# Decode attention and feed-forward on one core: V of a row's last layer-0 pair used as the matmul's weight, and small PSUM results moved to the score and output banks around each turn

## The chip, the cores and the metric

The kernel runs on one core of one Trainium2 chip. The metric is the device time of one execution in microseconds.

The names used below: PE is TensorE, which multiplies; DVE is VectorE and ACT is ScalarE, which turn its results into the next inputs; PSUM is the memory into which PE writes, in banks of 512 columns. In a product one operand is the weight (`lhsT` in the code) and the other moves (`rhs`).

## The reference, cut to what matters

```python
# B = 8 rows, one query each, D = 640; 32 heads, 4096 cached keys, Dh = 128; Dff = 1728; bf16
x = x + A(layernorm(x))     # "layer 0": attention over the cache, then wo
x = x + F(layernorm(x))     #            feed-forward, relu
x = x + A(layernorm(x))     # "layer 1": the same weights and the same cache again
x = x + F(layernorm(x))
# A: q = x @ wq; p = softmax(q k^T * Dh**-0.5); (p v) @ wo
```

The cache of one row is read twice, and layer 1 of a row can start only when its layer-0 feed-forward is done. 1 GB of K and V has to pass through the core's SBUF.

## The kernel before: the parts that matter

Heads are taken in pairs, 16 pairs per row and layer; one visit is one pair. A pair's K and V are four 512 KB units each. A planner in Python lays down one order of all instructions. An arena of 26 units holds what is loaded. At the end of a row's layer 0, 21 units are kept for layer 1 and three more are stashed, so that they are not read twice; loads near a turn therefore come as single units, issued as units come free. Two pairs of the next row are put between a row's last layer-0 pair and its first layer-1 pair, to give the feed-forward chain time (for the last row, two layer-1 pairs of the row before). I call that stretch the turn. There are eight.

```python
visits += nxt[:AHEAD] + cur + nxt[AHEAD:]         # AHEAD = 2: two pairs of the next row, then layer 1 of this one
...
# after the V products of visit i
ops.append(("OC", i))                             # ACT copies the output bank
step()                                            # at most 20 chain products between two units
chains.append([(6, ("OG", i)), (0, ("O", i))])    # gather; scale by 1/sum
if last_of[layer, b] == i and (layer == 0 or b == B - 1):
    chains[-1] += [(14, ("W", i)), (0, ("YC", i))] + finish(layer, b)
...
def finish(layer, b):     # layer 0: up x5, var, relu, down x5, add, mean, center, query, var2, query
```

Three PSUM banks do all the work; the other five hold the stash.

```python
o_ps = ps.tile([P, CJ * Dh], FP32, name="o_ps")       # output bank
s_ps = ps.tile([P, BANK], FP32, name="s_ps")          # score bank
small_ps = ps.tile([P, BANK], FP32, name="small_ps")  # everything else, by columns:
# oy_ps, sum_ps, mean_ps, var_ps, turn_ps, max_ps, q1_ps, lsum_ps, ffn_ps, P_ps

# do_mm, V: P is the weight, V moves (4 products of 512 columns per unit); only the very last visit has V as weight
nc.tensor.matmul(o_ps[32 * c : 32 * c + CJ, :], lhsT=P_tiles[i][:, h, j : j + CJ],
                 rhs=arena[:, at + c * CJ * Dh : at + (c + 1) * CJ * Dh], ...)
# do_mm, K around a turn: K is the weight, 16 products of one column per unit
s_tiles[i] = s_ps[:, i % 2 * 2 * NJ : (i % 2 + 1) * 2 * NJ]
```

## Time and profile before

| | before |
|---|---|
| median of the first three runs | 2345.71 us (2343.61 to 2347.46) |
| profiled span | 2343.2 us |
| bytes, mean rate | 988 MB, 423 GB/s |
| PE / DVE / ACT busy | 60% / 21% / 18% |

From the page of before: the span, the busy times, the rate in 40 equal slices, the chain that ended last by engine, and the group of ACT's output copies (count, busy us, mean ns, idle before).

```profile
span 2343.2 us, 42314 instructions
PE 1401.7 (60%) x18396; PEld 583.6 (25%) x18396; DVE 495.1 (21%) x2014; ACT 430.1 (18%) x994; POOL 59.6 (3%) x296
...
GB/s 411 430 432 402 431 431 432 431 407 435 430 431 428 412 434 433 432 426 409 431 435 430 423 409 436 429 432 415 416 434 431 432 410 424 431 431 431 393 433 330
...
DMA 70%; PE 18%; ACT 6%; DVE 4%; issue 2%; SPq 0%; DVEq 0%; ACTq 0%; POOL 0%; POOLq 0%
...
L787 ACT CAST o_sb<-o_ps 100x512 bf16<-100x512 f32 x255 | 149.4, 586 | 266.3 <-PE o_ps L679 265.5
```

The rate line is the one to look at. It is flat near 432 GB/s except for eight dips and the first and last slices: the loads bound the kernel, and the dips are the turns. Stretches of 20 us around the fourth turn (columns: busy us and count of PE, PEld, DVE, ACT, POOL; clock; DMA share; GB/s):

```profile
1020.00:1040.00 20.00, 13.46 (x142) 4.28 (x138) 4.43 (x17) 2.89 (x6) 0.00 (x0) 0.50 1.00 427
1040.00:1060.00 20.00, 14.10 (x263) 8.35 (x263) 8.38 (x35) 3.26 (x8) 0.00 (x0) 0.50 1.00 412
1060.00:1080.00 20.00, 16.08 (x342) 11.65 (x343) 4.74 (x28) 2.83 (x11) 4.88 (x23) 0.50 0.99 385
1080.00:1100.00 20.00, 15.47 (x310) 9.42 (x310) 5.86 (x25) 8.72 (x21) 0.00 (x0) 0.50 1.02 425
```

The DMA share stays near 1.00 while the rate falls to 385, so the share is no measure of loss here; the rate is. Summing (1 - rate/432) over the turns gives some 32 us in all.

What PE waits for in a turn, from the view of waits (who, line and tile it writes <- whom: us in total, times, longest us):

```profile
PE s_ps L697 <- ACT P_sb L753: 13.2, 14, 1.1
PE small_ps L572 <- DVE lsum L779: 2.5, 8, 0.3
PE small_ps L792 <- DVE xc L594: 1.8, 7, 0.3
PE small_ps L816 <- ACT qo L655: 1.7, 7, 0.2
PE small_ps L487 <- DVE s1h L481: 2.3, 7, 0.8
```

The last one is the mean's wait for its own input. Counts of 7 and 8 (and 14, twice per turn: 0.76 us in most turns and 1.09 us at the scores of a layer-1 pair just after) say that these come once per turn. The same waits in place, in the timeline of PE in the fourth turn (start us, us, what, and in brackets the idle before it and its releaser):

```profile
1063.86 0.57 PE L697 MATMUL s_ps<-qo,arena 128*128 128x1 bf16 x16 [0.76 <-ACT P_sb L753]
...
1069.51 0.60 PE L679 MATMUL o_ps<-arena,P_sb 128*4 128x512 bf16 x4
1070.04 0.23 PE L773 MATMUL small_ps<-P_sb,few 128*128 128x64 bf16 x1
1070.59 0.60 PE L572 MATMUL small_ps<-hT,w_sb 128*128 128x1 bf16 x14 [0.32 <-DVE lsum L779]
1071.12 0.60 PE L679 MATMUL o_ps<-arena,P_sb 128*4 128x512 bf16 x4
1071.97 0.36 PE L487 MATMUL small_ps<-s1h,few 128*128 128x1 bf16 x2 [0.25 <-DVE s1h L481]
1072.59 0.24 PE L792 MATMUL small_ps<-few,o_sb 100*128 100x2 bf16 x4 [0.26 <-DVE xc L594]
1072.76 0.60 PE L679 MATMUL o_ps<-arena,P_sb 128*4 128x512 bf16 x4
...
1074.16 0.41 PE L816 MATMUL small_ps<-oT,wo_sb 128*128 128x1 bf16 x10 [0.25 <-ACT qo L655]
1074.49 0.60 PE L679 MATMUL o_ps<-arena,P_sb 128*4 128x512 bf16 x4
1075.68 0.60 PE L679 MATMUL o_ps<-arena,P_sb 128*4 128x512 bf16 x4 [0.44 <-DMA arena<-in_A_kv_dram]
```

Each L679 line is one unit of V used, and so one unit of the arena given back to the loads. Units leave here every 1.2 to 1.7 us; at 432 GB/s a 512 KB unit takes 1.21 us. Look at the line at 1070.59: a down product of the feed-forward writes columns 392 to 396 of the small bank (the end of ffn_ps, behind the up products) and waits until DVE has read the softmax sums in columns 216 to 279 of the same bank. No value passes between them. That is the kind of wait the change is after.

### The profile page before, as it was taken

Reading aid. Unit: us, or ns where it says so; the run is one execution under the profiler, and the core shown is the slowest. Engines: PE = TensorE matmul, PEld = TensorE weight load, DVE = VectorE, ACT = ScalarE, POOL = GpSimd, SP = SyncE. Lnnn points to the kernel's source line nnn. Section 1 sums busy time; section 2 is a strip of 40 time slices with the busy share of each in tenths; the row PEclk is TensorE's granted clock in tenths of the full one; section 3 lists DMA queues with packets and bytes.
Section 4 is the critical chain, followed back from the end, with each engine's and each line's share of the span. In section 5 each row is a group of like instructions: output and inputs, shape, how many; then the busy total and the mean of one; then the engine's idle time right before and its main releaser. Section 6 shows DMA issues by size and latency. Waiting matters only on the chain.

```text
span 2343.2 us, 42314 instructions
## 1 busy us (share of the span) xinstructions
PE 1401.7 (60%) x18396; PEld 583.6 (25%) x18396; DVE 495.1 (21%) x2014; ACT 430.1 (18%) x994; POOL 59.6 (3%) x296
## 2 busy tenths in 40 slices
PE   3547655576555855557545685556755577555766
PEld 1214211142112511124111241113311133111523
DVE  1113211131112211122111221112211122111312
ACT  1111211122111221112111121111311112111211
POOL 0000000000000000000000000000000000000000
PEclk9999999999955555555555555555555555555555
DMA  9999999999999999999999999999999999999997
GB/s 411 430 432 402 431 431 432 431 407 435 430 431 428 412 434 433 432 426 409 431 435 430 423 409 436 429 432 415 416 434 431 432 410 424 431 431 431 393 433 330
DMA packets 75598, 990.82 MB, mean 423 GB/s; under 512 B 8468, under 2 KB 8468, under 8 KB 36372
## 3 DMA queue, kind: packets, MB, share of 16 engines
q1 hardware_dynamic: 75412, 988.12, 99.4%
q8 instruction: 143, 2.34, 0.4%
q14 instruction: 43, 0.35, 0.0%
HBM read 988.08 MB, written 0.01 MB: 422 GB/s over the span
## 4 chain that ended last, share of the span: by engine, by line
DMA 70%; PE 18%; ACT 6%; DVE 4%; issue 2%; SPq 0%; DVEq 0%; ACTq 0%; POOL 0%; POOLq 0%
DMA arena<-in_A_kv_dram 70%; PE o_ps L679 5%; PE s_ps L687 4%; PE s_ps L697 3%; ACT P_row L747 2%; PE small_ps L647 1%; ACT o_sb L787 1%; DVE mrow L705 1%; ACT P_sb L753 1%; PE small_ps L792 1%; ACT arena L626 1%; PE small_ps L760 1%; PE small_ps L816 1%; ACT nmax L745 1%; DVE hmx L724 0%
## 5 line engine op out<-in xcount | busy, mean ns | idle before, releaser
L679 PE MATMUL o_ps<-arena,P_sb 128*4 128x512 bf16 x4080 | 598.6, 596 | 407.2 <-DMA arena<-in_A_kv_dram 405.5
L687 PE MATMUL s_ps<-arena,qz 128*4 128x512 bf16 x3040 | 409.7, 601 | 255.9 <-DMA arena<-in_A_kv_dram 245.0
L679 PEld LDWEIGHTS <-P_sb 128*4 128x4 bf16 x4080 | 111.1, 88 | 533.1 <-issue 517.4
L705 DVE TENSOR_REDUCE mrow<-s_ps 100x1 bf16<-100x512 f32 x190 | 131.9, 694 | 354.7 <-PE s_ps L687 354.7
L787 ACT CAST o_sb<-o_ps 100x512 bf16<-100x512 f32 x255 | 149.4, 586 | 266.3 <-PE o_ps L679 265.5
L745 ACT ACTIVATE nmax<-small_ps 100x1 f32<-100x1 f32 x106 | 18.2, 171 | 798.6 <-PE small_ps L734 798.6
L697 PE MATMUL s_ps<-qo,arena 128*128 128x1 bf16 x4224 | 141.3, 165 | 33.9 <-DMA arena<-in_A_kv_dram 17.8
L697 PEld LDWEIGHTS <-arena 128*128 128x128 bf16 x4224 | 129.7, 104 | 50.6 <-DMA arena<-in_A_kv_dram 33.7
L767 DVE CAST P_sb<-small_ps 128x64 bf16<-128x64 f32 x190 | 42.6, 224 | 466.1 <-PE small_ps L760 466.1
L687 PEld LDWEIGHTS <-qz 128*4 128x4 bf16 x3040 | 62.1, 84 | 305.0 <-issue 286.1
L760 PE MATMUL small_ps<-few,P_row 100*128 100x16 bf16 x760 | 52.4, 180 | 96.7 <-ACT P_row L747 96.7
L745 ACT ACTIVATE nmax<-small_ps,q_scale 100x1 f32<-100x1 f32 x84 | 21.9, 261 | 410.8 <-PE small_ps L734 410.8
L779 DVE TENSOR_REDUCE lsum<-small_ps 128x2 f32<-128x64 f32 x256 | 57.5, 225 | 167.8 <-PE small_ps L773 167.8
L719 DVE TENSOR_REDUCE diag<-small_ps 1x2 bf16<-1x16 f32 x190 | 30.8, 162 | 276.9 <-PE small_ps L712 273.2
L760 PEld LDWEIGHTS <-P_row 100*128 100x128 bf16 x760 | 35.2, 108 | 191.9 <-ACT P_row L747 187.1
L647 PE MATMUL small_ps<-xq,wq_sb 128*128 128x1 bf16 x1280 | 51.9, 165 | 40.3 <-DVE qo L807 33.5
L792 PEld LDWEIGHTS <-o_sb 100*128 100x128 bf16 x1020 | 47.9, 107 | 109.0 <-ACT o_sb L787 78.4
L792 PE MATMUL small_ps<-few,o_sb 100*128 100x2 bf16 x1020 | 67.2, 170 | 10.9 <-DVE xc L594 1.8
L747 ACT ACTIVATE P_row<-s_ps,nmax 100x512 bf16<-100x512 f32 x106 | 72.9, 687 | 3.4
L712 PE MATMUL small_ps<-few,mrow 100*1 100x16 bf16 x190 | 35.7, 188 | 55.5 <-DVE mrow L705 55.5
L647 PEld LDWEIGHTS <-wq_sb 128*128 128x128 bf16 x1280 | 53.2, 104 | 53.4 <-issue 51.7
L747 ACT ACTIVATE P_row<-s_ps,nmax,q_scale 100x512 bf16<-100x512 f32 x84 | 65.3, 777 | 2.8
(212 smaller groups left out, 854.6 us busy)
## 6 DMA issues: line engine op xcount, KB each, us to landing
arena<-in_A_kv_dram SPq DMA_DIRECT2D x126, 4096.0 KB, 23.1
arena<-in_A_kv_dram SPq DMA_DIRECT2D x89, 2048.0 KB, 20.4
arena<-in_A_kv_dram SPq DMA_DIRECT2D x218, 512.0 KB, 6.1
arena<-in_A_kv_dram SPq DMA_DIRECT2D x16, 3072.0 KB, 22.0
arena<-in_A_kv_dram SPq DMA_DIRECT2D x38, 1024.0 KB, 10.6
arena<-in_A_kv_dram SPq DMA_DIRECT2D x10, 2560.0 KB, 19.9
arena<-in_A_kv_dram SPq DMA_DIRECT2D x15, 1536.0 KB, 20.5
wq_sb<-in_A_wq_dram SPq DMA_DIRECT2D x4, 1280.0 KB, 17.6
```

The lines of the kernel that those rows point to most:

```text
L647: nc.tensor.matmul(q_ps[:, h : h + 1], lhsT=wq_sb[:, g, c, (2 * n + h) * Dh : (2 * n + h + 1) * Dh], rhs=xlns[b][:, 0, c : c + 1], start=( ...
L679: nc.tensor.matmul(o_ps[32 * c : 32 * c + CJ, :], lhsT=P_tiles[i][:, h, j : j + CJ], rhs=arena[:, at + c * CJ * Dh : at + (c + 1) * CJ * D ...
L687: nc.tensor.matmul(s_ps[32 * c : 32 * c + CJ, :], lhsT=qz[:, i % 3, c // 2, 3 - g : 3 - g + CJ], rhs=arena[:, at + c * BANK : at + (c + 1) ...
L697: nc.tensor.matmul(s_tiles[i][:, j : j + 1], lhsT=arena[:, at + n * P : at + (n + 1) * P], rhs=qo[:, b, h : h + 1], start=True, stop=True,)
L705: nc.vector.tensor_reduce(out=m_tiles[i][:OR, :1], in_=s_ps[:OR], axis=AX.X, op=ALU.max)
L745: nc.scalar.activation(out=nm[:OR, :1], in_=max_ps[:OR, :1], func=ACT.Copy, scale=less)
L747: nc.scalar.activation(out=P_rows[i][:OR], in_=s_ps[:OR], func=ACT.Exp, bias=nm[:OR, :1], scale=more)
L760: nc.tensor.matmul(P_ps[:, k * 4 * CJ : (k + 1) * 4 * CJ], lhsT=P_row[:OR, k * P : (k + 1) * P], rhs=rsel[:OR], start=True, stop=True,)
L767: nc.vector.tensor_copy(out=P_tiles[i].rearrange("p h (c k) -> p h c k", k=BANK // P), in_=P_ps.rearrange("p (k h c) -> p h c k", k=BANK / ...
L779: nc.vector.tensor_reduce(out=L, in_=lsum_ps.rearrange("p (h j) -> p h j", h=2), axis=AX.X, op=ALU.add)
L787: nc.scalar.copy(out=o_tiles[i][:OR], in_=o_ps[:OR, :].rearrange("p (j d) -> p j d", j=CJ))
L792: nc.tensor.matmul(oy[i][:, :2], lhsT=o_tiles[i][:OR, j, :], rhs=gsel[:OR, j, :], start=(j == 0), stop=(j == CJ - 1))
```

## The change

Its intent is to free PE in the turn. V of a row's last layer-0 pair becomes the weight, so that its output lands in one column per head and needs no ACT copy and no gather: the finishing chain starts one step earlier. And results that all lived in the small bank go to banks that rest in the turn: scores of the first of the two pairs ahead to the output bank; softmax sums of both, mean, variance and the turn's first query to the score bank. The core of the diff:

```diff
+    direct = [i == NV - 1 or visits[i][0] == 0 and last_of[visits[i][:2]] == i for i in range(NV)]
+    ahead = [next((t - i for t in turns if 0 < t - i <= AHEAD), 0) for i in range(NV)]
 ...
-            if i < NV - 1:
+            if not direct[i]:
                 ops.append(("OC", i))
                 step()
                 chains.append([(6, ("OG", i)), (0, ("O", i))])
 ...
+    lsum2_ps = s_ps[:, 4 * NJ : 6 * NJ]
+    mean2_ps, var2_ps, q2_ps = (s_ps[:, 6 * NJ + lo : 6 * NJ + hi] for lo, hi in ((0, 1), (1, 2), (2, 4)))
+    o2_ps = o_ps[:, :1], s_ps[:, 8 * NJ - 1 : 8 * NJ]
 ...
-            over_partitions(mean_ps[:, :1], st.pop("s1"))
+            over_partitions(mean2_ps, st.pop("s1"))
 ...
-        q_ps = st["q", b, hp] = q1_ps[:, 2 * (hp % 2) : 2 * (hp % 2) + 2]
+        q_ps = st["q", b, hp] = q2_ps if hp == NP - 1 else q1_ps[:, 2 * (hp % 2) : 2 * (hp % 2) + 2]
 ...
-                for n in range(CJ) if i == len(visits) - 1 else ():
+                for n in range(CJ) if direct[i] else ():
                     nc.tensor.matmul(
-                        (s_ps if h else o_ps)[:, :1], lhsT=arena[...], rhs=P_tiles[i][:, h, j + n : j + n + 1],
+                        o2_ps[h], lhsT=arena[...], rhs=P_tiles[i][:, h, j + n : j + n + 1],
 ...
-            s_tiles[i] = s_ps[:, i % 2 * 2 * NJ : (i % 2 + 1) * 2 * NJ]
+            s_tiles[i] = o_ps[:, 2 * NJ : 4 * NJ] if ahead[i] == AHEAD else s_ps[:, i % 2 * 2 * NJ : (i % 2 + 1) * 2 * NJ]
 ...
-            lsum_ps, lhsT=ones_p, ...
+            lsum2_ps if ahead[i] else lsum_ps, lhsT=ones_p, ...
 # cut: the center, root2, clear, reading of the sums and scaling of the output follow the new places
```

More of the change, by code (lines that the diff above doesn't have):

```diff
@@ L281, in plan @@
     assert at[0] == len(stream) and not any(owner) and not weights
-    return visits, moving, ops
+    return visits, moving, direct, ahead, ops
 def _free(ap: bass.AP, shape_strides) -> bass.AP:
@@ L419 @@
     up_parts = [range(f, min(f + 3, FC)) for f in range(0, FC, 3)]
-    visits, moving, ops = plan(B, NP, len(up_parts), DC)
+    visits, moving, direct, ahead, ops = plan(B, NP, len(up_parts), DC)
     s_tiles, P_rows, P_tiles, m_tiles, o_tiles, oy, invL, oT, nmax, st = ({} for _ in range(10))
@@ L550, in var, with var2 @@
             over_partitions(var_ps[:, :nb], st.pop("s2"))
+        def var2():
+            over_partitions(var2_ps, st.pop("s2"))
         def root():
@@ L594, in center @@
             nc.vector.scalar_tensor_tensor(
-                out=xc, in0=_free(mean_ps[:, :1], [(1, 1), (0, DC)]), scalar=-1.0 / D, in1=x, op0=ALU.mult, op1=ALU.add
+                out=xc, in0=_free(mean2_ps, [(1, 1), (0, DC)]), scalar=-1.0 / D, in1=x, op0=ALU.mult, op1=ALU.add
             )
@@ L602, in root2 @@
             r = q_scale[b] = sm.tile([P, 2], FP32, name="q_scale", bufs=2)
-            inverse_root(r[:, 0:1], var_ps[:, :1], float(Dh))
+            inverse_root(r[:, 0:1], var2_ps, float(Dh))
             nc.gpsimd.tensor_scalar(out=r[:, 1:2], in0=r[:, 0:1], scalar1=-1.0, scalar2=None, op0=ALU.mult)
-        return dict(up=up, var=var, root=root, relu=relu, down=down, add=add, mean=mean, center=center, var2=var, root2=root2)
+        return dict(up=up, var=var, root=root, relu=relu, down=down, add=add, mean=mean, center=center, var2=var2, root2=root2)
     xlns, q_scale, finishing = {}, {}, {}
@@ L661, in do_clear @@
     def do_clear():
-        nc.vector.memset(s_ps[:, : 4 * NJ], -1e30)
+        nc.vector.memset(s_ps[:, : 8 * NJ], -1e30)
     def do_mm(which, i, g, u):
@@ L670, in do_mm @@
                 h, j = c // 2, g * VJ + c % 2 * CJ
-                for n in range(CJ) if i == len(visits) - 1 else ():
+                for n in range(CJ) if direct[i] else ():
                     nc.tensor.matmul(
-                        (s_ps if h else o_ps)[:, :1], lhsT=arena[:, at + (c * CJ + n) * Dh : at + (c * CJ + n + 1) * Dh],
+                        o2_ps[h], lhsT=arena[:, at + (c * CJ + n) * Dh : at + (c * CJ + n + 1) * Dh],
                         rhs=P_tiles[i][:, h, j + n : j + n + 1],
@@ L676, in do_mm @@
                     )
-                if i == len(visits) - 1:
+                if direct[i]:
                     continue
@@ L773, in do_l @@
         nc.tensor.matmul(
-            lsum_ps, lhsT=ones_p, rhs=P_tiles[i].rearrange("p h j -> p (h j)"), start=True, stop=True
+            lsum2_ps if ahead[i] else lsum_ps, lhsT=ones_p, rhs=P_tiles[i].rearrange("p h j -> p (h j)"), start=True, stop=True
         )
@@ L779, in do_i @@
         nc.vector.tensor_reduce(
-            out=L, in_=lsum_ps.rearrange("p (h j) -> p h j", h=2), axis=AX.X, op=ALU.add
+            out=L, in_=(lsum2_ps if ahead[i] else lsum_ps).rearrange("p (h j) -> p h j", h=2), axis=AX.X, op=ALU.add
         )
@@ L799, in do_o @@
             dst = qo[:, b, 2 * hp : 2 * hp + 2]
-            if i == len(visits) - 1:
-                oy[i] = oy_ps[:, : 2 + DC * B]
-                for h, o in enumerate((o_ps, s_ps)):
-                    nc.vector.tensor_tensor(out=dst[:, h : h + 1], in0=o[:, :1], in1=invL[i][:, h : h + 1], op=ALU.mult)
-                return
         else:
             dst = oT[i] = sm.tile([P, 2], BF16, name="oT")
-        nc.vector.tensor_tensor(out=dst, in0=oy[i][:, :2], in1=invL.pop(i), op=ALU.mult)
+        L = invL.pop(i)
+        if not direct[i]:
+            nc.vector.tensor_tensor(out=dst, in0=oy[i][:, :2], in1=L, op=ALU.mult)
+            return
+        oy[i] = oy_ps[:, : 2 + DC * B]
+        for h, o in enumerate(o2_ps):
+            nc.vector.tensor_tensor(out=dst[:, h : h + 1], in0=o, in1=L[:, h : h + 1], op=ALU.mult)
     def do_w(i):
```

## The prediction

> **What bounds it now.** The load of K and V. The page's DMA part shows 988 MB in 2343 us, 423 GB/s; the chain that ended last is 70% DMA into the arena; PE is busy 60%. The stage table (20 us stretches) shows 425 to 440 GB/s everywhere except around the eight turns from a row's layer 0 to its layer 1 and the last 15 us. The Trainium skill (DMA: Bandwidth & Descriptors, "Where 436 GB/s comes from") puts the ceiling at 435 GB/s, and the calm stretches agree. At a turn the rate falls to 377 to 412 GB/s for some 40 us. Summing (1 - rate/432) over those stretches, one turn loses 3.1 to 5.5 us, all eight about 32 us. That bounds the gain: 1.4%.
>
> **Why a turn loses.** Most of the arena holds kept units, so loads are single 512 KB units, issued as PE releases one. DMA delivers one per 1.2 us. In the timeline of one turn (1055 to 1077 us) PE first waits for DMA (0.2 to 0.8 us per unit, until 1062); then, until 1076, units follow at about 1.4 us, because PE also does the feed-forward matmuls (0.6 us per unit) and waits for other engines. The same waits in each turn: 0.76 us of a score product for ACT's exp (reads the other columns of the score bank), 0.32 of a down product for DVE's sum, 0.25 for the sum of the mean, 0.25 of the output gather for DVE's center, 0.25 of an output projection for ACT's query copy. The skill (PSUM — Partial Sum Buffer, "PSUM bank collisions raise a hardware error") says two engines must not touch one bank and quadrant at once; the trace agrees: most waits are for readers of other columns.
>
> **What the change does, per turn.**
> - V of the last layer-0 pair as weight: 16 matmuls of one column per unit, about 0.57 us (score products, same form) against 0.60 now: nothing. It removes the 0.59 us ACT copy and the gather (0.27 us PE, 0.18 wait), and moves the finishing chain one step earlier. PE then waits for DMA, so little counts.
> - First following pair's scores in the output bank: removes the 0.76 us wait; adds a wait of about 0.35 us for DVE's read of the output bank before those scores (in the DMA-bound part).
> - Softmax sums in the score bank: removes 0.32; may add about 0.35, as the sum matmul must now wait for the maximum over the scores.
> - Mean and first query in the score bank: removes 0.25 + 0.25; the mean's own wait stays.
> Net in the PE-bound part: 0.76 + 0.32 + 0.50 - 0.35 = 1.2 us, of which I expect 0.8 to 1.0 to reach the loads, since PE meets DMA again before the turn (a 0.44 us wait). Eight turns: about 7.5 us.
>
> **Predicted: 2338 us (-0.33%), range 2330 to 2344. Faster by over 2%: 1%; within 2%: 98%; slower by over 2%: 1%.**
>
> **What would show it.** The waits of PE for the exp fall from 14 to about 7 (13.2 to about 7.5 us); those for lsum, center and query copy in turns vanish; ACT's output copies fall from 255 to 247; turn stretches gain about 10 GB/s each. Wrong step: a new wait of PE for the max (score bank) or for the last output in each turn.
>
> **What would make it wrong.** Turns limited by the landing latency of single units rather than PE (then about 0 to 3 us); the shifted chain changes the load schedule, either way by some us; or the earlier chain lets all units flow at 1.2 us (then up to 15 us).

## The result, and the profile after

| | before | after |
|---|---|---|
| median of six runs each | 2348.16 us | 2341.61 us (2339.39 to 2344.78) |
| ratio, 95% interval | | 0.9976 [0.9964, 0.9989] |
| the same, five more rounds (a1_repeat) | 2348.18 us | 2340.34 us, 0.9969 [0.9956, 0.9981] |

A ratio is the mean time of one kernel's runs over that of the other's in the same rounds, so it is not quite the ratio of the medians quoted beside it.

The change is faster by 0.24 to 0.31%, some 6 to 7 us. The profiled execution after (2344.78 us on the device clock) is the slowest of its six. The profiled one before (2344.99 us) is a seventh execution, faster than five of its six. So the two spans agree by accident. A single pair of traces can't show a gain of 0.3%; what it can show is which waits are there. From the page after:

```profile
span 2343.0 us, 43024 instructions
PE 1398.6 (60%) x18748; PEld 591.4 (25%) x18748; DVE 496.7 (21%) x2022; ACT 426.3 (18%) x986; POOL 59.5 (3%) x296
...
GB/s 411 430 433 401 433 432 432 431 396 432 432 432 430 404 434 431 430 427 403 433 432 431 426 412 434 430 432 420 427 431 427 432 416 430 431 431 431 396 433 329
...
DMA 71%; PE 17%; ACT 6%; DVE 3%; issue 2%; SPq 0%; POOL 0%; ACTq 0%; DVEq 0%; POOLq 0%
...
L795 ACT CAST o_sb<-o_ps 100x512 bf16<-100x512 f32 x247 | 144.9, 587 | 289.3 <-PE o_ps L687 286.0
```

Eight output copies are gone (255 to 247). The dips are still there. The same stretches:

```profile
1020.00:1040.00 20.00, 10.15 (x108) 3.37 (x100) 3.59 (x14) 2.89 (x6) 0.00 (x0) 0.50 0.99 426
1040.00:1060.00 20.00, 12.87 (x266) 7.63 (x266) 8.41 (x32) 2.67 (x7) 0.00 (x0) 0.50 1.00 417
1060.00:1080.00 20.00, 15.89 (x330) 11.38 (x327) 4.83 (x29) 2.77 (x10) 4.60 (x22) 0.50 0.99 374
1080.00:1100.00 20.00, 15.37 (x348) 10.35 (x347) 5.61 (x24) 7.46 (x18) 0.28 (x2) 0.50 1.03 416
```

This one turn of this slow-end execution is no better than before, 374 against 385. The waits of PE after:

```profile
PE s_ps L705 <- ACT P_sb L761: 7.6, 7, 1.1
PE s_ps L492 <- DVE lsum L787: 2.6, 8, 0.4
PE small_ps L549 <- ACT nmax L757: 2.2, 8, 0.4
PE o_ps L705 <- DVE oT L816: 0.2, 1, 0.2
```

The waits for the center (xc) and the query copy are gone; the wait for the exp is halved; the wait for the sums is as long as before but now falls on the mean (L492). The order does this and not the new bank: with the chain one step earlier, the mean is the next product after the sums in their bank. The run a4 below, with both in the small bank, has the same wait (2.5 us, 8 times), and b4, without the earlier chain, doesn't have it. In place, the fourth turn:

```profile
1071.10 0.60 PE L687 MATMUL o_ps<-arena,P_sb 128*4 128x512 bf16 x4
1071.63 0.62 PE L580 MATMUL small_ps<-hT,w_sb 128*128 128x1 bf16 x14
1073.45 0.60 PE L687 MATMUL o_ps<-arena,P_sb 128*4 128x512 bf16 x4 [1.20 <-DMA arena<-in_A_kv_dram]
1073.98 0.23 PE L781 MATMUL s_ps<-P_sb,few 128*128 128x64 bf16 x1
1074.53 0.19 PE L492 MATMUL s_ps<-s1h,few 128*128 128x1 bf16 x2 [0.32 <-DVE lsum L787]
1074.74 0.59 PE L687 MATMUL o_ps<-arena,P_sb 128*4 128x512 bf16 x4
...
1075.76 0.60 PE L687 MATMUL o_ps<-arena,P_sb 128*4 128x512 bf16 x4
...
1076.98 0.59 PE L687 MATMUL o_ps<-arena,P_sb 128*4 128x512 bf16 x4 [0.20 <-DMA arena<-in_A_kv_dram]
1077.50 0.42 PE L655 MATMUL small_ps<-xq,wq_sb 128*128 128x1 bf16 x10
1078.21 0.59 PE L687 MATMUL o_ps<-arena,P_sb 128*4 128x512 bf16 x4 [0.28 <-DMA arena<-in_A_kv_dram]
```

From 1074.74 on units leave every 1.0 to 1.2 us, as fast as the loads bring them, and PE waits for DMA again. Taken over the eight turns, between the product of the last pair's output with the summed output weights (tile `wo_sum`, 1057.07 us in before) and the first layer-1 score product, the idle times printed in PE's timeline add up per turn to 1.84 us for ACT and DVE and 1.2 us for DMA before, and to 0.70 us and 2.6 us after (0.74 and 2.4 in a1_repeat). So 1.1 us per turn of waiting for engines went, 9 us in all; most of it turned into waiting for data, which is what one sees when PE is pushed off the path of the loads.

### The profile page after: what moved, and what is told of

Its sections match the earlier page's. It is cut to its first block, busy times and chain, and to the rows that moved or that the text cites. A ratio compares the mean times of both kernels' runs of the same rounds, so it can differ in the third digit from the quotient of the medians.

```text
span 2343.0 us, 43024 instructions
## 1 busy us (share of the span) xinstructions
PE 1398.6 (60%) x18748; PEld 591.4 (25%) x18748; DVE 496.7 (21%) x2022; ACT 426.3 (18%) x986; POOL 59.5 (3%) x296
## 4 chain that ended last, share of the span: by engine, by line
DMA 71%; PE 17%; ACT 6%; DVE 3%; issue 2%; SPq 0%; POOL 0%; ACTq 0%; DVEq 0%; POOLq 0%
DMA arena<-in_A_kv_dram 71%; PE o_ps L687 5%; PE s_ps L695 4%; PE s_ps L705 2%; ACT P_row L755 2%; ACT o_sb L795 1%; PE small_ps L655 1%; DVE mrow L713 1%; ACT P_sb L761 1%; PE small_ps L800 1%; ACT arena L634 1%; PE small_ps L768 1%; PE small_ps L825 1%; DVE hmx L732 0%; ACT nmax L753 0%
## 5 line engine op out<-in xcount | busy, mean ns | idle before, releaser
L687 PE MATMUL o_ps<-arena,P_sb 128*4 128x512 bf16 x3952 | 584.3, 596 | 402.0 <-DMA arena<-in_A_kv_dram 401.0
L705 PE MATMUL s_ps<-qo,arena 128*128 128x1 bf16 x3712 | 123.7, 165 | 17.2 <-ACT P_sb L761 7.6
L720 PEld LDWEIGHTS <-mrow 100*1 100x1 bf16 x190 | 15.0, 79 | 210.8 <-DVE mrow L713 210.8
```

The costliest lines, as they stand in the source:

```text
L705: nc.tensor.matmul(s_tiles[i][:, j : j + 1], lhsT=arena[:, at + n * P : at + (n + 1) * P], rhs=qo[:, b, h : h + 1], start=True, stop=True,)
L720: nc.tensor.matmul(turn_ps[:1, : 4 * CJ], lhsT=m[:OR, :1], rhs=rsel[:OR], start=True, stop=True)
```

## The experiments

Each run was timed in five rounds against the kernel before on the same chip: the a and c runs on one chip, the b runs on another. A difference between a b run and the others is thus one of two ratios, each to before on its own chip. A ratio's 95% interval is about 0.0013 to each side, 3 us; differences between two variants below that are not decided by the ratios alone.

Theory A is the prediction's: removed PE waits in the turn let units come free earlier, the exp wait being the largest term. Rivals: B, the planner's clock no longer counts the gather and so draws up another load schedule (513 loads become 521, and only 56 keep their place, slot and size), and that is the gain; C, V as weight and the earlier chain carry it; D, as C for the exp wait, which makes the score move idle; E, only the end of the chain counts; F, the turns are bound by the landing of single units and PE matters little.

### a1_repeat: the changed kernel again

No edit.

> The changed kernel again, for a tighter interval and a second trace. Expected 0.9970 to 0.9985 of before (2340 to 2345 us).

Measured: 2340.34 us, 0.9969 [0.9956, 0.9981]. The gain stands, near 7 us, at the edge of the expected range (0.0001 below it).

### a2_new_compute_old_loads and a3_old_compute_new_loads: compute and load schedule exchanged

The order of the products is the same in both kernels, so the memory operations (loads, stash, weights) between two products can be taken from one plan and the rest from the other. The first is:

```diff
     visits, moving, direct, ahead, ops = plan(B, NP, len(up_parts), DC)
+    ops = spliced(ops, plan(B, NP, len(up_parts), DC, old=True)[-1])   # products and slots, loads, stash: old plan; the rest: new
```

and the second is the kernel before with the loads of the new plan in the same way.

> The changed kernel's computing instructions in their order, with the load schedule (sizes, slots, places between the products) of before. Theory A (the removed PE waits carry the gain): 0.9965 to 0.9982, as the change. Rival B (the gain comes from the load schedule that the planner draws up when the gather leaves its clock): 0.9992 to 1.0008, no gain.

> The computing instructions of before, with the load schedule of the changed kernel. Theory A: 0.9992 to 1.0010. Rival B: 0.9965 to 0.9985, as the change.

Measured: new compute with old loads 2340.26 us, 0.9969 [0.9957, 0.9982], the same as the full change; old compute with new loads 2346.79 us, 0.9999 [0.9986, 1.0011], nothing. Rival B falls. The load schedule changed nearly everywhere and is worth nothing; the computing instructions carry the whole gain, within the intervals.

### a4_direct_only: V as weight alone

```diff
-    ahead = [next((t - i for t in turns if 0 < t - i <= AHEAD), 0) for i in range(NV)]
+    ahead = [0] * NV
-    mean2_ps, var2_ps, q2_ps = (s_ps[...] ...)
+    mean2_ps, var2_ps = mean_ps[:, :1], var_ps[:, :1]
-        q_ps = st["q", b, hp] = q2_ps if hp == NP - 1 else q1_ps[...]
+        q_ps = st["q", b, hp] = q1_ps[...]
```

> The changed kernel with V of the last layer-0 pair as weight, but scores, softmax sums, mean and first query where they were before. Theory A (the bank moves free PE in the turn; V as weight alone does little where PE waits for DMA): the 0.76 us waits for the exp come back, 0.9988 to 1.0005. Rival C (V as weight and the earlier finishing chain carry it): 0.9965 to 0.9985.

Measured: 2345.23 us, 0.9984 [0.9970, 0.9998]. This is half of the gain by the ratio: just inside the range of rival C (0.9985 at most) and outside that of theory A (0.9988 at least), but the interval reaches both. The trace decides one point. From its waits of PE, and from its timeline in the fourth turn:

```profile
PE s_ps L705 <- ACT P_sb L761: 7.6, 7, 1.1
PE small_ps L655 <- DVE oT L812: 5.2, 16, 0.4
PE small_ps L549 <- ACT nmax L757: 2.2, 8, 0.3
...
1065.56 0.63 PE L549 MATMUL small_ps<-xf,w_sb 128*128 128x1 bf16 x10 [0.26 <-ACT nmax L757]
1066.12 0.59 PE L705 MATMUL s_ps<-qo,arena 128*128 128x1 bf16 x16
```

The exp wait fell from 13.2 to 7.6 us without any score having moved. Theory A said it would come back. Because the chain runs one step earlier, an up product of the feed-forward (L549) now stands before the score product; it waits 0.26 us for ACT's scaled maximum, and by the time the score product comes, ACT's exp is done. That ACT no longer copies the output is not the cause: in before it had been idle for 7.3 us when this maximum came (1063.14 us). New waits took some of it back: the second line had 9 entries and 2.7 us before, it has 16 and 5.2 here.

### b1_before_again: before against itself

No edit.

> The kernel before against itself: what the comparison shows when nothing differs, and a trace of before from the same chip. Expected 0.9990 to 1.0010.

Measured: 2347.75 us, 0.9998 [0.9984, 1.0012]. The comparison is sound to its interval. Its trace (span 2345.8 us) is nearer to before's median than the first one.

### b2_without_score_move, b3_without_small_moves, b4_small_moves_only: the parts of the change

```diff
 # b2, from the changed kernel
-            s_tiles[i] = o_ps[:, 2 * NJ : 4 * NJ] if ahead[i] == AHEAD else s_ps[...]
+            s_tiles[i] = s_ps[...]
 # b3, from the changed kernel: lsum2, mean2, var2, q2 back to lsum_ps, mean_ps, var_ps, q1_ps
 # b4, from the changed kernel: as b2, and
-    direct = [i == NV - 1 or visits[i][0] == 0 and last_of[visits[i][:2]] == i for i in range(NV)]
+    direct = [i == NV - 1 for i in range(NV)]
```

> The changed kernel, but the scores of the first following pair stay in the score bank. Theory A as predicted (the 0.76 us wait for the exp is the largest term of the saving): that wait comes back in every turn, and half of the gain goes: 0.9978 to 0.9990. Rival D (once V is the weight the chain comes a step earlier and the wait for the exp is gone anyway, as in the run with V as weight alone): the full gain, 0.9962 to 0.9976.

> The changed kernel, but softmax sums, mean, variance and first query stay in the small bank (V as weight and the score move are kept). Theory A: 0.9976 to 0.9988. Rival D: as V as weight alone, 0.9980 to 0.9990; a loss in the loads 10 to 20 us after the first down product as large as before.

> The kernel before with only the sums, mean, variance and first query moved to the score bank (no V as weight, no score move). If the parts add up: 0.998 to 0.999 (about half of the gain). If the moves need V as weight to be of use: 0.9993 to 1.0007.

| kernel | V as weight | score move | small moves | median us | ratio, 95% |
|---|---|---|---|---|---|
| b1 | | | | 2347.75 | 0.9998 [0.9984, 1.0012] |
| a4 | x | | | 2345.23 | 0.9984 [0.9970, 0.9998] |
| b3 | x | x | | 2342.89 | 0.9978 [0.9966, 0.9991] |
| b4 | | | x | 2341.58 | 0.9973 [0.9961, 0.9986] |
| b2 | x | | x | 2341.69 | 0.9970 [0.9956, 0.9984] |
| a1 | x | x | x | 2340.34 | 0.9969 [0.9956, 0.9981] |

Without the score move the gain is whole (b2, inside the range of D), and its exp wait is 7.6 us as in the changed kernel (first line below). So theory A's largest term is wrong and D is right: in the presence of V as weight the score move has nothing left to remove. What the score move does by itself was not run. b3 lies in the range of theory A and 0.0002 below that of D, which does not separate them; its loss 10 to 20 us after the first down product is as large as before (10.3 us, last table), as D said. The small moves alone give most of the gain (b4), more than either expectation for them allowed (0.998 at most), while the exp wait stays at 13.2 us in that kernel (second and third lines):

```profile
PE s_ps L705 <- ACT P_sb L761: 7.6, 7, 1.1
...
PE s_ps L705 <- ACT P_sb L761: 13.2, 14, 1.1
PE s_ps L492 <- DVE s1h L486: 0.8, 1, 0.8
```

In b4 the waits of a down product for the sums, of the gather for the center and of the projection for the query copy, 2.5 + 1.8 + 1.7 us before, are not in the list. A fourth went too, which the prediction had expected to stay: the mean's wait for its own input fell from 7 times and 2.3 us to once and 0.8 us. So removing the 0.76 us wait was not needed for a gain: waits of 0.25 to 0.32 us late in the turn gave 0.27% in b4. That this is more than the 0.16% of a4, where the 0.76 us wait went, is not decided by the intervals. The parts do not add: 0.16% for V as weight and 0.27% for the small moves make 0.43%, and the whole is 0.31%. By their intervals that is not decided, but the last two experiments suggest why it should be so.

### c1_sums_only and c2_mean_query_only: the small moves taken apart

From b4, with one half put back each: c1 keeps `lsum2_ps` and returns mean, variance and query to the small bank; c2 the other way round.

> The kernel before with only the softmax sums of the two pairs ahead of a turn in the score bank. It takes away one 0.32 us wait of a down product per turn. Theory A, each removed wait counted at its length: 8 x 0.32 = 2.6 us, 0.9989 (0.9980 to 0.9998). Rival E (the early wait does not matter, only the end of the finishing chain, which the query of the turn waits for): 0.9995 to 1.0005.

> The kernel before with only mean, variance and first query in the score bank. It takes away 0.26 and 0.25 us per turn. Theory A: 8 x 0.5 = 4 us, 0.9983 (0.9972 to 0.9993). Rival E: nearly all of what the two moves gave together (0.9973): 0.9968 to 0.9980.

Measured: sums only 2344.86 us, 0.9987 [0.9973, 1.0001]; mean, variance and query only 2342.17 us, 0.9977 [0.9964, 0.9989]. Theory A's ranges hold in both: 3.1 and 5.4 us by the ratios, where it had counted 2.6 and 4. But the traces show that the counts behind these ranges were not what happened. In c1 the mean's wait for its input went too (2.3 to 0.8 us), some 4 us in all. In c2 the projection waits for DVE's output where it had waited for the query copy:

```profile
PE small_ps L825 <- DVE oT L812: 4.1, 8, 2.4
PE small_ps L580 <- DVE lsum L787: 2.5, 8, 0.3
```

The first was once and 2.4 us before, and the second is as before. So the listed waits of c2 fell by only some 1.6 us in all, less than its interval allows for the gain (2.6 to 8.5 us). What shortened the turn more is that the gather no longer waits for the center, and so not for the mean's product to end: in the fourth turn the next V unit starts 0.39 us after the mean's product does (1072.75 and 1073.14 us), 0.79 us in before (1071.97 and 1072.76), and the first seven turns agree to 0.01 us. Eight times 0.40 us is 3.2 us, an estimate inside the interval. So removing a listed wait of 0.26 us shortened this stretch by 0.40 us. Rival E's ranges were 0.9995 to 1.0005 and 0.9968 to 0.9980; the second holds and the first doesn't, but c1's interval reaches 1.0001, so E stays open.

### c3_old_ffn_cut and c4_new_ffn_cut: how much PE could give at all

```diff
-                for c in range(DC):                     # up
+                cs = range(1 if layer == 0 else DC)
+                for c in cs:
-            for c, f in [(k, f) for f in range(FC)] if layer == 0 else ...   # down
+            for c, f in [(k, f) for f in range(3)] if layer == 0 else ...
```

Wrong results on purpose (relative error 0.83). The layer-0 feed-forward of a row falls from 140 products to 29 (the expectation below says 135; the timeline shows 70 up and 70 down). Ten to fifteen of them take 0.5 to 0.6 us, so this is about 4 us of PE per turn. The bytes stay.

> Wrong result on purpose: before, with the layer-0 feed-forward products of each row cut from 135 to 29, about 4 us less of PE work in each turn; the DMA bytes stay. Theory A (PE's pace in the turn sets when units come free): a clear gain beyond that of the change, 0.9935 to 0.9965. Rival F (landing latency of single units sets the pace, PE matters little): 0.9975 to 1.0000.

> Wrong result on purpose: the same cut in the changed kernel; it shows what PE still costs there. Theory A: the change took a part only, so 0.9930 to 0.9962, a further 0.1% or more below the changed kernel. If the change has already brought PE out of the way: 0.9962 to 0.9976, no more than the changed kernel.

Measured: 2339.93 us, 0.9966 [0.9954, 0.9979] for the old kernel cut; 2338.50 us, 0.9964 [0.9951, 0.9976] for the new one cut. The first lies outside both of its ranges: 0.0001 above that of theory A, and below that of rival F, so PE does matter, but the clear gain beyond that of the change, which theory A expected, is not there. The old kernel gains 0.34% from 4 us less work per turn, 32 us of PE in all, hardly more than the change got by removing 9 us of waits. The new kernel gains next to nothing on top of the change (0.9964 against 0.9969, inside the range for a PE that is already out of the way). So PE's pace in the turn is worth about 8 us (5 to 11 by the interval), and by the middle values the change has taken nearly all of that. This would explain why the parts do not add: either of them soon meets the same ceiling. What the turns still lose is not PE's feed-forward.

### Where in the turn the gain is

From each trace I took the rate in stretches placed by the first down product of every turn, and summed (1 - rate/432) x length over the eight turns: us of load time lost. These are one execution each.

```
stretch, us from the first down product    -25..0   0..10   10..20   20..45   all
before                                       14.4     6.6     10.3      0.8   32.1
b1_before_again                              13.6     6.7     13.1      0.9   34.2
a3 old compute, new loads                    13.7     6.4     11.4      1.0   32.7
a4 V as weight alone                         13.8     6.6     10.7      1.5   32.5
b3 V as weight and score move                13.5     7.2     10.3      1.1   32.0
c1 sums alone                                14.6     7.1      9.2      1.0   31.8
c2 mean, variance, query alone               13.6     7.1      8.0      0.9   29.6
b4 small moves alone                         14.6     7.5      8.0      0.7   30.8
b2 without the score move                    14.3     6.6      6.6      1.4   28.9
a2 new compute, old loads                    14.0     6.9      6.7      1.0   28.7
after                                        15.4     6.1      8.7      1.2   31.4
a1 the change again                          14.0     8.1      5.5      1.7   29.3
c3 old, feed-forward cut                     12.3     4.9      8.2      0.7   26.1
c4 new, feed-forward cut                     13.6     5.7      6.4      1.1   26.9
```

Of the kernels with the full feed-forward, those with the old places for the small results lose 10.3 to 13.1 us between 10 and 20 us after the first down product; those with new ones lose 5.5 to 9.2. Two traces of one kernel differ by up to 3.2 us there (8.7 and 5.5), so the groups count (means 11.2 and 7.5 us) and not single lines. Before that stretch they differ by up to 2 us in no such order.

One more reading of the table: take the last column from the span of the same execution, and 2310.8 to 2311.7 us are left in all fourteen (2343.2 - 32.1 in before, 2340.8 - 29.3 in a1, 2337.0 - 26.1 in c3). Outside the turns nothing changed, then, by more than 1 us: the gain, and also the scatter between traces of one kernel, lie in the eight turns. The waits removed at 5 to 9 us show in the loads a few us later, as they should: a unit given back late is a load issued late, and single-unit loads land a median of 6.1 us after their issue (the DMA part of the page before).

## Why the prediction was right, and where it was not

The forecast was 2338 us, -0.33%, in a range of 2330 to 2344. Measured: 2341.61 us, 0.9976 at first, 0.9969 in the repeat. Direction, size, class and the mechanism as a whole (PE's waits in the turn delay the release of units) were right; the largest term of the sum was not, and that the sum came out is in part luck. In absolute terms the median sits 3.6 us above the forecast, of which about 2.5 us is that before itself measured 2348.16 rather than 2345.71 in the same rounds.

Step by step:

- "The load of K and V" bounds, and turns lose 32 us: held (32.1 and 34.2 us in two traces of before). "That bounds the gain" was a loose bound: the cut feed-forward shows that PE can give about 8 us of it.
- V as weight: "PE then waits for DMA, so little counts". Wrong: it is what halved the exp wait. Alone it measured 0.16% [0.02, 0.30].
- "First following pair's scores in the output bank: removes the 0.76 us wait". This is the step that failed. The wait does go (13.2 to 7.6 us, as forecast), but it goes by the earlier chain; without the score move the gain is 0.9970 and the wait is gone all the same.
- "Softmax sums in the score bank: removes 0.32; may add about 0.35". The added wait for the maximum was not there: a down product stands between. But the wait for the sums did not vanish: in the kernels with V as weight it falls on the mean (2.6 us over 8 turns).
- "Mean and first query: removes 0.25 + 0.25": held in the full change. Alone (c2) it gained 5.4 us, though the second of the two waits was replaced by one of 0.26 us for DVE's output.
- The net of 1.2 us per turn: 1.1 us in the traces. 0.8 to 1.0 of it reaching the loads, 7.5 us: 5.6 to 7.3 us. The sum was right although its largest term belonged to another part: the 0.35 us that was to be added for the maximum over the scores did not come, and 0.26 us for ACT's maximum at an up product, which is not in the prediction, came instead. That these cancel is luck.
- The wait before the scores for DVE's read of the output: predicted 0.35 us, seen once at 0.2 us, since PE waits for data there.
- "Turn stretches gain about 10 GB/s each": not visible in single traces of 20 us stretches; the rate of one stretch scatters by more.

Not settled: whether the score move is worth exactly nothing (b3 against a4, and a1 against b2, differ by 0.0006 and 0.0001, both inside the intervals and both across the two chips), and what the remaining loss in the turns (29.3 and 31.4 us in the two traces of the change, 26.9 with the cut) is made of. Landing latency with only five spare units is a candidate; I did not test it.

## What to carry to other kernels

When a load-bound kernel has short stretches in which an engine's pace decides when buffers come free, removing waits there pays only until that engine meets the loads again; cut its work by a large amount once, wrong result and all, to learn the ceiling before counting single waits. In this kernel, two results in one PSUM bank made PE wait for the reader of the other one even where their columns are disjoint (0.25 to 0.32 us each, gone in b4 when the banks were changed), so it pays to try different banks for results that are read at the same time. And a list of waits is not a list of gains: the longest of them vanished by itself when the chain moved by one step.

## What the Trainium skill lacked or had wrong

- "PSUM — Partial Sum Buffer", section "PSUM bank collisions raise a hardware error", says that two engines must be kept off one bank and quadrant, and the waits here agree (a down product waits for DVE's read of other columns). It has no price for it: here 0.25 to 0.32 us per small result and 0.76 to 1.09 us for an exp over the scores; moving mean, variance and one query to another bank was worth 0.23% [0.11, 0.36] of the run.
- "DMA: Bandwidth & Descriptors", section "Where 436 GB/s comes from", says that for loads from HBM a limit near 358 GB/s per core binds. That sentence leaves out its condition, that both cores of a pair load, which the skill gives in other places. Here one core alone loaded 431 to 432 GB/s in every long stretch between turns, close to the same section's fabric figure of 435.
- The same page's rule under "Measured (HBM→SBUF, 128 partitions, SWDGE, issued from GpSimd)" asks for 1 MiB or more per transfer for 75% of the peak. Here 512 KB loads (issued from SP) came 1.22 to 1.24 us apart in the fourth turn of before (starts of the score products that waited for them: 1056.35, 1057.58, 1058.80, 1060.04 us), about 426 GB/s worked out from that. The rule's table has no line for 512 KB loads that follow each other.
- No page has a figure for how little the busy share of the DMA engines tells of the rate: in the fourth turn of before it stays at 0.99 while the rate falls from 432 to 385 GB/s, and in the other turns it is 0.97 to 1.02.
